# Attention and a two-part mixture of experts on one core: the second layer's first weights loaded behind the sixth head pair's keys, with new instruction orders for the attention part

## The chip, the core and the metric

The kernel runs on one core of a Trainium2 chip. The core has a matrix engine (PE, or TensorE), a vector engine (DVE), a scalar engine (ACT), GpSimd (POOL) and SyncE (SP), whose queue here issues nearly all DMA transfers. Each engine works through its own list in order; semaphores hold an instruction until what it needs is there. The metric is the device time of one execution in microseconds (us).

## The reference

What is computed, cut to what matters:

```
scores = scale * q @ k.T                       # 2 batches, 8 heads, 576 tokens, 64 per head
scores = where(0 <= i - j < 128, scores + bias, -1e9)   # a sliding window with slopes per head
attn = softmax(scores);  x = (attn @ v) laid out as [1152, 512]
out = 0                                        # first mixture: 4 experts, 512 -> 1024 -> 512
for e in range(4):
    out += p[:, e:e+1] * (relu(x @ w1[e]) @ w2[e])
xn = out / rms(out) * rms_g                    # second block: gate, value, out
return (silu(xn @ w_gate) * (xn @ w_val)) @ w_out       # 512 -> 1536 -> 512
```

All of it is in float32; most matrix products are done as three products of a rounded high part and a low part (the remainder).

## The kernel before, in words

The program has two parts. The first is the attention with some of the first expert's work between; the second is all the rest, ordered by a planner (`Plan`). The change touches the first part alone, and the instructions of the second part stand in the same order on every engine in both kernels.

Attention goes by head pairs, numbered 0 to 7 (four of batch 0, then four of batch 1). A pair's steps are:

- `load` (line 392): SP issues the pair's queries and keys (lines 403, 404) into one of two `qt`/`kt` buffers, and with every second pair the values of two pairs (lines 409, 410). A pair's buffers are those of the pair two before it, so the transfer waits until that pair's last scores are done.
- scores on PE (line 483), three pieces a pair; masked minimum on DVE (503); exponential on ACT (509); sums turned into factors on DVE (526, 527, once for three rows of blocks); scaling of each block on POOL (532), nine a pair.
- transposes on PE (550), copies of them out by DVE or ACT (388, 390), products with the values on PE (569 and 580).
- `halves` (597): ACT writes the high part, DVE the low part of the result.

Between these stand the first weights of the two layers of expert 0. `weights` (610) loads two transfers of 512 KB into the two buffers `raw` (`load_raw`, 260). ACT writes a high part of each half (388), and POOL or DVE the low part (629), so a layer has four low parts, two for each `raw` buffer. The second layer's two loads need the `raw` buffers back: the first after low parts 1 and 2 of the first layer, the second after low parts 3 and 4.

As soon as batch 0 is done, products of the first layer (654) and then of the second (685) fill PE between the transposes of batch 1.

What sets the order: `Flow` (line 151). Every operation is added with its possible engines, a cost and its needs. A string for each engine (`ORDERS`: d DVE, a ACT, p POOL, t PE) says which kind comes next there; `SHARED` says which engine takes an operation that two could do. SP's loads stand in the order in which they were added. `Flow.run` walks the strings with the costs and emits the operations by the start times that it finds; the hardware then holds each engine to the list that comes out.

In `weights`, a load is told to need `prev["w"]`, which is the second low part of the layer before, and then only for the first of the two loads (line 621 sets it to nothing). The second load is given no need.

Of the kernel before, what the change touches and what calls it, by code (L numbers as in the profile page):

```python
# [150 lines left out]
class Flow:  # L151
# [17 lines left out]
    def run(self, orders, shared):  # L169
# [30 lines left out]

ORDERS = {
    "d": (
        "bbbbmmmmmmmrmmmrmmmrmcmrcmmmcrmmmrmlmmmhrmmmcrcmrcmclmhcmrmmmrmmmcmmrclhmcmmmrcmmmmrmhlmummcmrWrummu"
        "rmcmcmurcmmmmrluuruumhucWmmmprumgummrcgmmlhyrmgrcclgucuhyculh"
    ),
    "a": (
        "mmmmmmmmmmmmmmmcmmcmmhlmmcmcmmmmmmmwlhwmmcmmmcmmhlwmmwmcmcmmhlmmmmwmmmwvwmmmmvmucvmwmmmvlhmcmvmvmmcc"
        "umvvgcmumglmmgmhmgmcmclcyhccuhlyvv"
    ),
    "p": "BnnnnnnnnnBnnnBnnnnnnnnnnnnnnWWnnnnnnnnnnWWnnnnnnnnnnnnnnnnWnnnnnnnnnnWnnnnnnnnnn",  # L210
    "t": (
        "ssssssxsxxoxxooozsxxssxxoooxxozssxxoosxxooxzssxxooxxsoozssxfffsfxffxfxfxsoooozssxfffxfxffxfxfoooozss"
        "xggggxgxgxgxgoooozxgxgxggxgxgoooozggkjkj"
    ),
}
SHARED = {
    "B": "ppp",
    "W": "ppppdpdp",
    "c": "ddadaaadddddaadddaadddddaadaaadaaddaadda",
    "y": "dada",  # L220
}


# [1 line left out]
def tile_fused(ctx: ExitStack, tc: tile.TileContext, qS, kS, vS, probs, w1, w2, wgv, wo, g, out):  # L225
# [19 lines left out]
    def slot_a():  # L245
        return wpa.tile([P, 2, 512], F32R, tag="wa", name="wa")
# [11 lines left out]
    def load_raw(src):  # L258
        raw = wraw.tile([P, 2, 512], F32, tag="raw", name="raw")
        nc.sync.dma_start(out=raw, in_=src)  # L260
        return raw
# [50 lines left out]
    def load_probs():  # L312
        nc.sync.dma_start(out=pr_sb, in_=probs)

    def norm_probs():
        nc.vector.tensor_reduce(out=psm, in_=pr_sb, op=ALU.add, axis=mybir.AxisListType.X)
        nc.vector.tensor_scalar(out=psm, in0=psm, scalar1=1e-9, scalar2=None, op0=ALU.add)
        nc.vector.reciprocal(out=psm, in_=psm)
        nc.vector.tensor_tensor(out=pn_sb, in0=pr_sb, in1=psm.to_broadcast([P, NTT, E]), op=ALU.mult)

    y = ypool.tile([P, NTT, DM], F32, tag="y", name="y")
# [18 lines left out]
    with (  # L340
# [38 lines left out]
        order = [(b, p) for b in range(B) for p in range(H // 2)]  # L379
        flow = Flow({"t": 3.9, "d": 1.6, "a": 2.9, "p": 4.15, "q": 0.7})  # L380
        add = flow.add
        qts, kts, vts, sts, pts, pes, pos = {}, {}, {}, {}, {}, {}, {}
        sps, psts, raws = {}, {}, {}
        did = {}

        def copied(e, out, in_):
            if e == "a":
                nc.scalar.activation(out=out, in_=in_, func=AF.Copy)
            else:
                nc.vector.tensor_copy(out, in_)  # L390
# [4 lines left out]
        def load(n):  # L395
            b, p = order[n]

            def both(e):
                if n not in qts:
                    qts[n] = qk_p.tile([P, S], F32, tag="q", name="qt")  # L400
                    kts[n] = qk_p.tile([P, S], F32, tag="k", name="kt")
                for c in ((slice(0, FIRST), slice(FIRST, S)) if n == 0 else (slice(0, S),)):
                    (nc.scalar if n == 0 else nc.sync).dma_start(out=qts[n][:, c], in_=qS[b, p, :, c])
                    nc.sync.dma_start(out=kts[n][:, c], in_=kS[b, p, :, c])

            def values(e):
                vt = v_p.tile([P, 5, 4 * D], F32, tag="v", name="vt")
                hs = slice(p * P - P, p * P - P + 4 * D)
                nc.sync.dma_start(out=vt[:, :4, :], in_=vS[b, : 4 * P, hs].rearrange("(k p) d -> p k d", p=P))
                nc.sync.dma_start(out=vt[:D, 4, :], in_=vS[b, 4 * P :, hs])  # L410
                vts[n - 1] = vts[n] = vt

            hold, took = (2.0, 3.9) if n == 0 else (1.5, 3.5)
            did["qk", n] = add("q", "q", (hold, took), [did.get(("s", n - 2, 8))], both)
            did["qa", n] = did["qk", n]
            if n == 0:
                did["qa", 0] = add("q", "q", (0.0, 1.3), [], lambda e: None)
            if p % 2:
                did["v", n - 1] = did["v", n] = add("q", "q", (1.5, 3.7), [did.get(("o", n - 4, 4)), did.get(("o", n - 3, 4))], values)
            if n == 0:  # L420
                for i in range(2):
                    for r in range(2):
                        rows = slice(r * D, (r + 1) * D)

                        def slopes(e, rows=rows, r=r, i=i):
                            nc.vector.tensor_scalar(
                                out=bias[rows, 0, i, :], in0=rel[rows], scalar1=-8.0 * 2.0 ** (-8.0 * ((r ^ i) + 1) / H),
                                scalar2=1.0, op0=ALU.mult, op1=ALU.mult,
                            )

                        did["b", 0, r, i] = add("b", "d", (0.33, 0.4), [did["rel", r]], slopes)
            elif b == 0:

                def steeper(e):
                    EN[e].tensor_scalar(
                        out=bias[:, p, :, :], in0=bias[:, p - 1, :, :], scalar1=2.0 ** (-16.0 / H),
                        scalar2=1.0, op0=ALU.mult, op1=ALU.mult,
                    )

                cost = {"d": (0.48, 0.55), "p": (0.75, 0.8)}  # L440
                j = add("B", "dp", cost, [did["b", p - 1, r, i] for r in range(2) for i in range(2)], steeper)
                for r in range(2):
                    for i in range(2):
                        did["b", p, r, i] = j
# [168 lines left out]
        def weights(name, srcs, behind):  # L613

            made, ends = blocks.setdefault(name, []), []
            for i, src in enumerate(srcs):
                def fetch(e, i=i, src=src):
                    raws[name, i] = load_raw(src)

                j = add("q", "q", (1.35, 3.7), [behind, prev["w"]], fetch)  # L620
                prev["w"] = None
                for k in range(2):
                    def high(e, i=i, k=k):
                        made.append(slot_a())
                        copied(e, made[2 * i + k][:, 0, :], raws[name, i][:, k, :])

                    def low(e, i=i, k=k):
                        w = made[2 * i + k]
                        EN[e].tensor_tensor(out=w[:, 1, :], in0=raws[name, i][:, k, :], in1=w[:, 0, :].bitcast(F32), op=ALU.subtract)

                    ja = add("w", "a", (0.52, 0.62), [j, prev["wa"]], high)
                    prev["wa"] = ja
                    ends.append(add("W", "dp", {"p": (1.25, 1.29), "d": (0.62, 0.7)}, [ja], low))
            prev["w"] = ends[1]
            return ends

        def bank_of(rota):
# [94 lines left out]
            keep(3, 0, [j4])  # L732

        prev = dict.fromkeys("sxowf")
        prev["wa"] = None
        load(0)
        for n in range(len(order)):
            if n + 1 < len(order):
                load(n + 1)
            for ts in SCORES:  # L740
                scores(n, ts)
                for t in ts:
                    softmax(n, t)
            for t0 in range(0, NQ, 3):
                norm(n, t0, t0 + 3)
            for kb in range(5):
                values(n, kb)
            halves(n)
            if n == 2:
                did["w1"] = weights("w1_0", [w1[0, 0], w1[0, 1]], did["qk", 3])  # L750
                j = add("q", "q", (0.5, 3.5), [did["qk", 3]], lambda e: load_probs())
                did["pn"] = add("p", "d", (0.7, 0.8), [j], lambda e: norm_probs())
            if n == 3:
                did["w2"] = weights("w2_0", [w2[0, :, :2, :], w2[0, :, 2:, :]], did["qk", 4])
                x0 = [did[w, i] for w in ("ld", "hd") for i in range(4)]
                hid = [hidden_filler("ff", c, t0, (x0 + did["w1"], [])) for c in range(4) for t0 in (0, HT)]
                for t in range(4):
                    out_filler(t, hid)
                sums(x0, hid[-1])
# [36 lines left out]
    def add(e, out, a, b):  # L796
        EN[e].tensor_tensor(out=out, in0=a, in1=b, op=ALU.add)  # L797
# [410 lines left out]
    w, v = blocks.pop("w1_0"), blocks.pop("w2_0")  # L1208
# [18 lines left out]
    v = [((lambda x=x: x), End(0.0)) for x in v]  # L1227
# [66 lines left out]
    for u in range(1, NU):  # L1294
        w, w_read = nxt
# [130 lines left out]
    for e in (ET.PE, ET.DVE, ET.Activation, ET.Pool, ET.SP):  # L1426
        prev = None
        for i in traced[mark : listed if e == ET.SP else None]:
            if i.engine == e:
# [5 lines left out]
                prev = i  # L1435
# [32 lines left out]
```

## Time and profile before

| | us |
|---|---|
| median of 3 runs (lowest, highest) | 663.32 (661.49, 663.57) |
| the profiled execution, its own time | 663.5 |
| its span, first to last instruction | 661.7 |
| PE busy in the span | 647.8 (98%) |
| DVE busy | 509.0 (77%) |
| ACT busy | 314.9 (48%) |
| POOL busy | 45.8 (7%), all in the first 80 us |

The span is one execution taken by the profiler. Its own time is 1.8 us longer, since it holds what lies before the first and behind the last instruction. A matmul's end is modelled, so that gaps between the starts tell more than busy time. The granted clock is the share of full speed that the throttle gave PE: 1.00 is 2.4 GHz and 0.50 is 1.2 GHz.

### The profile page before, as it was taken

What the parts mean: (1) busy time and instruction counts of PE and PEld (TensorE: products, weight loads), DVE (VectorE), ACT (ScalarE), POOL (GpSimd) and SP (SyncE); (2) the same over time, 40 slices, a digit from 0 to 9 for tenths busy, and PEclk for the clock granted to TensorE, in tenths of its full rate; (3) what the DMA queues carried; (4) which work ended last, traced back from release to release, by engine and by line L of the source; (5) the groups of instructions that cost most, each with busy time, mean ns of one, the idle gap of its engine ahead of it and who ended that gap; (6) DMA issues with size and microseconds to landing.
All of it is one profiled execution on the core that took longest, in us unless ns stands there. A gap on an engine that the chain in (4) does not pass through costs nothing.

```text
span 661.7 us, 11029 instructions
## 1 busy us (share of the span) xinstructions
PE 647.8 (98%) x4166; PEld 583.8 (88%) x4166; DVE 509.0 (77%) x1116; ACT 314.9 (48%) x722; POOL 45.8 (7%) x95
## 2 busy tenths in 40 slices
PE   8879999999999999999999999999999999999997
PEld 5568798988989989989989889879998999889986
DVE  7858758688888888888888888889677378857672
ACT  7957555552543634625544534864355334313330
POOL 7735300000000000000000000000000000000000
PEclk9979999999999999999999999999999999999999
DMA  8251103324452543644515434012101201001012
GB/s 275 88 198 34 33 1 108 115 96 144 144 175 96 188 140 95 216 126 139 189 47 194 134 95 160 33 41 86 65 33 60 68 1 64 23 11 33 33 49 95
DMA packets 24229, 64.95 MB, mean 98 GB/s; under 512 B 2672, under 2 KB 5488, under 8 KB 24176
## 3 DMA queue, kind: packets, MB, share of 16 engines
q1 hardware_dynamic: 23888, 63.96, 29.9%
q8 instruction: 32, 0.52, 0.3%
q10 hardware_dynamic: 288, 0.30, 0.1%
q14 instruction: 21, 0.17, 0.1%
HBM read 52.45 MB, written 11.80 MB: 97 GB/s over the span
## 4 chain that ended last, share of the span: by engine, by line
PE 96%; DMA 2%; DVE 1%; POOL 1%; SPq 0%; issue 0%; ACT 0%; POOLq 0%
PE ps_a L1167 14%; PE ps_c L1049 11%; PE ps_d L1049 11%; PE ps_d L1167 9%; PE ps_c L1167 9%; PE ps_b L1167 8%; PE ps_b L1049 8%; PE ps_a L1049 8%; PE a L654 2%; PE ps_b L285 2%; PE ps_c L285 2%; PE ps_d L285 2%; PE ps_a L285 2%; PE pst L550 2%; PE po L569 2%; PE a L685 2%
## 5 line engine op out<-in xcount | busy, mean ns | idle before, releaser
L1167 PE MATMUL ps_a<-wa,op 128*128 128x512 f32 x396 | 93.8, 390 | 0.0
L1167 PEld LDWEIGHTS ps_a<-wa,op 128*128 128x128 f32 x396 | 74.2, 188 | 15.3
L801 ACT ACTIVATE op<-h 128x512 fp32r<-128x512 f32 x95 | 57.6, 626 | 59.5 <-PE ps_d L1167 24.7
L801 ACT ACTIVATE wb<-raw 128x512 fp32r<-128x512 f32 (+1 forms) x98 | 49.8, 536 | 39.5 <-DVE raw L794 39.4
L794 DVE TENSOR_TENSOR op<-h,op 128x512 fp32r<-128x512 f32 x95 | 63.7, 685 | 2.5 <-ACT op L801 2.2
L1167 PE MATMUL ps_c<-wa,op 128*128 128x512 f32 x252 | 59.1, 389 | 0.0
L1167 PE MATMUL ps_d<-wa,op 128*128 128x512 f32 x252 | 58.9, 389 | 0.0
L1167 PE MATMUL ps_b<-wa,op 128*128 128x512 f32 x240 | 56.6, 391 | 0.0
L794 DVE TENSOR_TENSOR wb<-raw,wb 128x512 fp32r<-128x512 f32 (+1 forms) x98 | 54.6, 576 | 2.1 <-ACT wb L801 1.7
L1167 PEld LDWEIGHTS ps_c<-wa,op 128*128 128x128 f32 x252 | 47.3, 188 | 9.8
L1167 PEld LDWEIGHTS ps_d<-wa,op 128*128 128x128 f32 x252 | 47.2, 188 | 9.8
L1167 PEld LDWEIGHTS ps_b<-wa,op 128*128 128x128 f32 x240 | 44.6, 188 | 9.1
L794 DVE TENSOR_TENSOR wa<-raw,wa 128x512 fp32r<-128x512 f32 (+1 forms) x50 | 32.0, 652 | 13.5 <-ACT wa L801 13.5
L1049 PE MATMUL ps_c<-xh,wb 128*128 128x288 f32 x160 | 38.6, 297 | 0.0
L1049 PE MATMUL ps_d<-xh,wb 128*128 128x288 f32 x160 | 38.6, 296 | 0.0
L1049 PE MATMUL ps_a<-xh,wb 128*128 128x288 f32 x160 | 38.3, 294 | 0.0
L1049 PE MATMUL ps_b<-xh,wb 128*128 128x288 f32 x160 | 38.2, 294 | 0.0
L801 ACT ACTIVATE wa<-raw 128x512 fp32r<-128x512 f32 (+1 forms) x50 | 28.0, 597 | 18.9 <-DMA raw<-in_w 16.5
L1110 ACT ACTIVATE h<-r 128x576 f32<-128x576 f32 x28 | 19.2, 685 | 30.9 <-DVE r L797 30.9
L797 DVE TENSOR_TENSOR r<-ps_c,x 128x288 f32<-128x288 f32 x44 | 20.1, 458 | 17.0 <-PE ps_c L1049 14.5
L794 DVE TENSOR_TENSOR raw<-raw 128x256 f32<-128x256 f32 x66 | 27.7, 419 | 0.7
L1049 PEld LDWEIGHTS ps_b<-xh,wb 128*128 128x128 f32 x160 | 27.8, 188 | 0.3
(264 smaller groups left out, 1531.6 us busy)
## 6 DMA issues: line engine op xcount, KB each, us to landing
raw<-in_w SPq DMA_DIRECT2D x32, 512.0 KB, 3.8
scratch<-in_wgv SPq DMA_DIRECT2D x24, 512.0 KB, 4.4
f<-stage SPq DMA_DIRECT2D x36, 256.0 KB, 2.5
raw<-f SPq DMA_DIRECT2D x18, 512.0 KB, 3.2
scratch<-in_wo SPq DMA_DIRECT2D x12, 512.0 KB, 4.6
out_y<-acc SPq DMA_DIRECT2D x9, 256.0 KB, 2.0
vt<-in_vS SPq DMA_DIRECT2D x4, 512.0 KB, 6.0
qt<-in_qS SPq DMA_DIRECT2D x7, 288.0 KB, 3.3
```

What stands on the lines that cost most here:

```text
L285: nc.tensor.matmul(ps, lhsT=a, rhs=x[:, k, tok], start=(n == 0), stop=(n == 3 * KC - 1))
L550: nc.tensor.transpose(pst[:w, j, :], tts[n % 2][:, 2 * kb + j, c0 : c0 + w], ident)
L569: nc.tensor.matmul(po[r, kb * P : kb * P + len(range(blocks.shape[1])) * P], lhsT=vt[:, kb, v], rhs=blocks[:, :, 1:3, :] if j else blocks[ ...
L654: nc.tensor.matmul(box[0], lhsT=a, rhs=x[:, k, tok], start=k == 0 and a is wh and x is xh, stop=k == 3 and a is wl)
L685: nc.tensor.matmul(box[0], lhsT=tile[0][:, x, k, :], rhs=v[:, i, :], start=k == 0 and x == i == 0, stop=k == 3 and x == 1)
L794: EN[e].tensor_tensor(out=out, in0=a, in1=b, op=ALU.subtract)
L797: EN[e].tensor_tensor(out=out, in0=a, in1=b, op=ALU.add)
L801: nc.scalar.activation(out=out, in_=a, func=AF.Copy)
L1049: nc.tensor.matmul(ps, lhsT=s[:, k, :], rhs=t(k), start=start and m == 0, stop=m == 5, skip_group_check=True,)
L1110: return wrote(gr, pl.now("a", tok.stop - tok.start, needs + was_reading[gr], lambda e: nc.scalar.activation(out=h[:, c, tok], in_=src, fu ...
L1167: nc.tensor.matmul(ps, lhsT=a(s)[:, k, :], rhs=w[k][0]()[:, i, :], start=(n == 0), stop=(n == 11))
```

## The change

Three things are done. The sixth pair's load (pair 5) is added ahead of the second layer's weights, and these get it as their `behind`. Both loads of the second layer are told of both low parts that free their buffer (`prev["w"][2 * i : 2 * i + 2]`). The loads of queries, keys and values are given longer times to landing (`took`), and the strings of all engines are others. Of the strings the first lines of two are shown.

```diff
@@ ORDERS, SHARED
-    "p": "BnnnnnnnnnBnnnBnnnnnnnnnnnnnnWWnnnnnnnnnnWWnnnnnnnnnnnnnnnnWnnnnnnnnnnWnnnnnnnnnn",
+    "p": "BBnnnnnnnnnBnnnnnnnnnnnnnnnnnnnnnWnnnWnnnWnnnnnnnnnnWnnnnnnnnnnnnnWnnnnnnnnnnnnn",
-    "W": "ppppdpdp",
+    "W": "pdpppddp",
...
@@ load
-            hold, took = (2.0, 3.9) if n == 0 else (1.5, 3.5)
+            hold, took = (2.0, 3.9) if n == 0 else (1.5, 4.4 if n == 1 else 4.1)
...
-                did["v", n - 1] = did["v", n] = add("q", "q", (1.5, 3.7), [did.get(("o", n - 4, 4)), did.get(("o", n - 3, 4))], values)
+                did["v", n - 1] = did["v", n] = add("q", "q", (1.5, 4.3), [did.get(("o", n - 4, 4)), did.get(("o", n - 3, 4))], values)
@@ weights
-                j = add("q", "q", (1.35, 3.7), [behind, prev["w"]], fetch)
-                prev["w"] = None
+                j = add("q", "q", (1.35, 3.7), [behind, *prev["w"][2 * i : 2 * i + 2]], fetch)
...
-            prev["w"] = ends[1]
+            prev["w"] = ends
@@ the loop over the pairs
-        prev["wa"] = None
+        prev["wa"], prev["w"] = None, []
         load(0)
         for n in range(len(order)):
-            if n + 1 < len(order):
+            if n + 1 < len(order) and n != 4:
                 load(n + 1)
+            if n == 3:
+                load(5)
+                did["w2"] = weights("w2_0", [w2[0, :, :2, :], w2[0, :, 2:, :]], did["qk", 5])
...
             if n == 3:
-                did["w2"] = weights("w2_0", [w2[0, :, :2, :], w2[0, :, 2:, :]], did["qk", 4])
                 x0 = [did[w, i] for w in ("ld", "hd") for i in range(4)]
```

SP's list, from pair 4's queries to pair 6's keys. In the kernel before, `qt_425` and `kt_426` are pair 4, `raw_495` and `raw_525` the second layer's weights, `qt_548`, `kt_549` pair 5, `vt_578` the values of pairs 4 and 5, `qt_601`, `kt_602` pair 6:

```order
L403 DMA qt_425<-in_qS 128x576
L404 DMA kt_426<-in_kS 128x576
L260 DMA raw_495<-in_w2 128x1024
L260 DMA raw_525<-in_w2 128x1024
L403 DMA qt_548<-in_qS 128x576
L404 DMA kt_549<-in_kS 128x576
L409 DMA vt_578<-in_vS 128x4x256
L410 DMA vt_578<-in_vS 64x256
L403 DMA qt_601<-in_qS 128x576
L404 DMA kt_602<-in_kS 128x576
```

The same stretch of SP's list in the changed kernel, where pair 5 is `qt_482`, `kt_483` with the values `vt_564`, the weights are `raw_588` and `raw_611`, and pair 6 is `qt_631`, `kt_632`:

```order
L403 DMA qt_452<-in_qS 128x576
L404 DMA kt_453<-in_kS 128x576
L403 DMA qt_482<-in_qS 128x576
L404 DMA kt_483<-in_kS 128x576
L409 DMA vt_564<-in_vS 128x4x256
L410 DMA vt_564<-in_vS 64x256
L260 DMA raw_588<-in_w2 128x1024
L260 DMA raw_611<-in_w2 128x1024
L403 DMA qt_631<-in_qS 128x576
L404 DMA kt_632<-in_kS 128x576
```

Four transfers of pair 5 have moved from behind the two weight transfers to a place ahead of them; pair 6's stand behind the weights in both.

POOL's list around pairs 2 to 4 in the kernel before; the `st` buffers tell the pairs apart (`st_321` is pair 2, `st_397` pair 3, `st_523` pair 4), and the rows of line 629 are the first layer's low parts, two for each of `raw_374` and `raw_399`:

```order
L532 TENSOR_SCALAR tt_122<-tt_122,st_321 128x192 x6
L629 TENSOR_TENSOR wa_441<-raw_374,wa_441 128x512
L629 TENSOR_TENSOR wa_468<-raw_374,wa_468 128x512
L532 TENSOR_SCALAR tt_122<-tt_122,st_321 128x192
L532 TENSOR_SCALAR y_87<-y_87,st_397 128x64
L532 TENSOR_SCALAR y_87<-y_87,st_397 128x128
L532 TENSOR_SCALAR y_87<-y_87,st_397 128x192 x7
L629 TENSOR_TENSOR wa_565<-raw_399,wa_565 128x512
L629 TENSOR_TENSOR wa_588<-raw_399,wa_588 128x512
L532 TENSOR_SCALAR tt_122<-tt_122,st_523 128x64
```

The same pairs in the changed kernel, where `st_320`, `st_391` and `st_538` are pairs 2, 3 and 4, and line 628 is line 629 of before:

```order
L532 TENSOR_SCALAR tt_122<-tt_122,st_320 128x192 x7
L532 TENSOR_SCALAR y_87<-y_87,st_391 128x64
L532 TENSOR_SCALAR y_87<-y_87,st_391 128x128
L532 TENSOR_SCALAR y_87<-y_87,st_391 128x192
L628 TENSOR_TENSOR wa_492<-raw_401,wa_492 128x512
L532 TENSOR_SCALAR y_87<-y_87,st_391 128x192 x3
L628 TENSOR_TENSOR wa_509<-raw_424,wa_509 128x512
L532 TENSOR_SCALAR y_87<-y_87,st_391 128x192 x3
L628 TENSOR_TENSOR wa_519<-raw_424,wa_519 128x512
L532 TENSOR_SCALAR tt_122<-tt_122,st_538 128x64
```

Three low parts of the first layer are left on POOL, and two of them now stand between the scalings of pair 3; the fourth has gone to DVE.

PE's list around pair 5's first scores (`kt_549`) in the kernel before, with the transposes of pair 3 (`y_87`) and its products (`pt_552`, `pe_553`):

```order
L569 MATMUL po_591<-pt_552,vt_347 64x256 x4
L550 MATMUL pst0_124<-ident_81,y_87 64x128
L550 MATMUL pst0_124<-ident_81,y_87 128x128 x2
L550 MATMUL pst1_125<-ident_81,y_87 64x128
L483 MATMUL s2_156<-kt_549,qt_548 64x64 x2
L483 MATMUL s0_154<-kt_549,qt_548 64x128 x2
L483 MATMUL s2_156<-kt_549,qt_548 64x192 x2
L483 MATMUL s0_154<-kt_549,qt_548 64x192 x2
L569 MATMUL po_591<-pt_552,vt_347 64x256 x2
L569 MATMUL po_591<-pt_552,vt_347 64x128 x2
L580 MATMUL pst1_125<-pt_552,vt_347 64x64 x2
```

The same place in the changed kernel, with `kt_483` for pair 5's keys and `pt_545` for pair 3:

```order
L569 MATMUL po_591<-pt_545,vt_369 64x256 x2
L550 MATMUL pst0_124<-ident_81,y_87 64x128
L550 MATMUL pst0_124<-ident_81,y_87 128x128 x2
L550 MATMUL pst1_125<-ident_81,y_87 64x128
L483 MATMUL s2_156<-kt_483,qt_482 64x64 x2
L483 MATMUL s0_154<-kt_483,qt_482 64x128 x2
L483 MATMUL s2_156<-kt_483,qt_482 64x192 x2
L483 MATMUL s0_154<-kt_483,qt_482 64x192 x2
L569 MATMUL po_591<-pt_545,vt_369 64x256 x4
L569 MATMUL po_591<-pt_545,vt_369 64x128 x2
L580 MATMUL pst1_125<-pt_545,vt_369 64x64 x2
```

Pair 5's first scores stand at the same place, but for two products of pair 3, which come behind them now.

## Rows read from the trace of the kernel before

**Rows 1.** The page, busy time of PE (share of the span, instructions).

```profile
PE 647.8 (98%) x4166; PEld 583.8 (88%) x4166; DVE 509.0 (77%) x1116; ACT 314.9 (48%) x722; POOL 45.8 (7%) x95
```

**Rows 2.** Waits of PE, 0 to 150 us: us in total, times, longest.

```profile
PE s L483 <- DMA kt<-in_kS: 7.5, 2, 6.3
PE s L483 <- DVE st L503: 0.6, 1, 0.6
```

**Rows 3.** Windows, 31 to 43 us: length, busy by engine, PEclk, DMA share, GB/s.

```profile
31.00:37.00 6.00, 0.00 (x0) 0.00 (x0) 0.56 (x4) 1.04 (x5) 1.07 (x3) 0.87 0.81 257
37.00:39.00 2.00, 1.95 (x20) 1.24 (x22) 0.68 (x5) 0.00 (x0) 0.00 (x0) 0.50 1.04 365
39.00:41.00 2.00, 2.00 (x28) 1.69 (x28) 1.09 (x7) 1.05 (x3) 1.23 (x3) 0.50 0.05 18
41.00:43.00 2.00, 2.00 (x20) 1.49 (x13) 1.44 (x6) 2.00 (x10) 0.00 (x0) 0.70 0.00 0
```

**Rows 4.** The chain of waits through the stall: start us, us, what.

```profile
28.40 2.49 POOL wa L629 x2
...
30.91 0.33 SPq L260
...
31.76 5.16 DMA kt<-in_kS
...
37.05 1.35 PE s L483 x12
38.40 1.48 PE po L569 x8
39.88 0.52 PE pst L580 x6
...
40.50 1.88 PE s L483 x18
42.38 0.56 PE pst L550 x4
```

**Rows 5.** The same chain elsewhere, at full clock.

```profile
20.61 0.32 PE pst L580 x6
...
21.63 0.32 PE a L483 x5
...
22.95 1.01 PE po L569 x8
23.96 0.70 PE s L483 x12
...
47.02 0.44 PE pst L550 x4
...
49.47 0.80 PE a L654 x6
...
65.37 0.97 PE s L483 x18
```

**Rows 6.** SP's queue in order of time: start us, us, what it issued.

```profile
23.66 7.57 SPq L260 DMA_DIRECT2D raw<-in_w  x2
31.33 0.38 SPq L403 DMA_DIRECT2D qt<-in_qS  x1
```

**Rows 7.** POOL in order of time, 21 to 31 us, idle before in brackets.

```profile
21.13 2.51 POOL L629 TENSOR_TENSOR wa<-raw,wa 128x512 fp32r<-128x512 f32 x2
...
27.17 1.23 POOL L532 TENSOR_SCALAR y<-y,st 128x192 f32<-128x192 f32 x3 [0.43 <-ACT xh L603]
28.36 2.52 POOL L629 TENSOR_TENSOR wa<-raw,wa 128x512 fp32r<-128x512 f32 x2
```

**Rows 8.** Lines 526 and 629: ns min/median/max, first and last start; one in time order.

```profile
L526 DVE TENSOR_SCALAR st<-st x24: 152/166/682, 6.8 to 72.0; 128x3 f32<-128x3 f32 x24
L629 POOL TENSOR_TENSOR wa<-raw,wa x6: 1267/1280/1702, 21.1 to 64.5; 128x512 fp32r<-128x512 f32 x6
...
30.22 0.68 DVE L526 TENSOR_SCALAR st<-st 128x3 f32<-128x3 f32 x1
```

More of the change, by code (lines that the diff above doesn't have):

```diff
@@ L202 @@
     "d": (
-        "bbbbmmmmmmmrmmmrmmmrmcmrcmmmcrmmmrmlmmmhrmmmcrcmrcmclmhcmrmmmrmmmcmmrclhmcmmmrcmmmmrmhlmummcmrWrummu"
-        "rmcmcmurcmmmmrluuruumhucWmmmprumgummrcgmmlhyrmgrcclgucuhyculh"
+        "bbbbmmmmmmmrmmrmmmmmrmmmccrrmmcmmmmcmmrmmlrmhrmcmmcrmmrmlmhccmrWccmmmmrlhmmmmrcmmmmrmhlmumruurmuumum"
+        "mmmrmrummWhlucumrcmprmWmmmmcgrgluhgmmcrmrmmccrlhcycucuguhul"
     ),
     "a": (
-        "mmmmmmmmmmmmmmmcmmcmmhlmmcmcmmmmmmmwlhwmmcmmmcmmhlwmmwmcmcmmhlmmmmwmmmwvwmmmmvmucvmwmmmvlhmcmvmvmmcc"
-        "umvvgcmumglmmgmhmgmcmclcyhccuhlyvv"
+        "mmmmmmmmmmmmmmmmmcmmmmmmlhcmmcmmmmcmmlhcmwmwwmwmmclhmmccmmcmmhmlmmwmmwvccmmvummvmccmmchmvmmlmmcwvuwv"
+        "mmvmcvmcgmmglgmhmmmcmygmmulhcchuylyvv"
     ),
-    "p": "BnnnnnnnnnBnnnBnnnnnnnnnnnnnnWWnnnnnnnnnnWWnnnnnnnnnnnnnnnnWnnnnnnnnnnWnnnnnnnnnn",
+    "p": "BBnnnnnnnnnBnnnnnnnnnnnnnnnnnnnnnWnnnWnnnWnnnnnnnnnnWnnnnnnnnnnnnnWnnnnnnnnnnnnn",
     "t": (
-        "ssssssxsxxoxxooozsxxssxxoooxxozssxxoosxxooxzssxxooxxsoozssxfffsfxffxfxfxsoooozssxfffxfxffxfxfoooozss"
-        "xggggxgxgxgxgoooozxgxgxggxgxgoooozggkjkj"
+        "ssssssxxssxxoooxxozsssxxoxxooozxsxxoooxxsxozssxxoxxsooozssxfxffffxfxffxsoooozssfxfxffxfxffxfxsoooozs"
+        "sgxgxggxggxoooozxggxgxgxgxoooozgggggkjkj"
     ),
@@ L217 @@
     "B": "ppp",
-    "W": "ppppdpdp",
-    "c": "ddadaaadddddaadddaadddddaadaaadaaddaadda",
-    "y": "dada",
+    "W": "pdpppddp",
+    "c": "ddaddaaddaaddddaaaadaaaaaaddadadadddadda",
+    "y": "adaa",
 }
```

## The prediction, made before the changed kernel ran

> **What bounds the kernel now.** I read the page first: PE is busy for 647.8 of the span's 661.7 us [rows 1], so no other engine bounds the whole, and what can be won is PE's 13.9 us of gaps and any time at a low clock. Next PE's waits [rows 2]: after the start there are 7.5 us for a transfer of keys, in two waits, the longest 6.3 us, and one of 0.6 us for DVE. Nothing later waits. Then the windows around the long wait [rows 3]: from 31 to 37 us PE does nothing, DVE, ACT and POOL almost nothing, and the DMA engines are 81% busy; from 37 to 41 PE works at a granted clock of 0.50, that is 1.2 GHz, and from 41 to 43 at 0.70 in the mean.
>
> The chain says why [rows 4]. POOL does two low parts of the first layer's weights, to 30.89. Then SP, which had stood at the second weight transfer of line 260, issues it, and behind it pair 5's queries and keys; the keys take 5.16 us to land, and pair 5's first scores start at 37.05. SP's own rows say the same [rows 6]: its two weight loads fill 23.66 to 31.23, since they wait for their buffers, and pair 5's queries are issued only at 31.33. So keys that depend on nothing but pair 3's last scores, done at 21.63 + 0.32 = 21.95 [rows 5], are 9.4 us late behind a transfer that nobody needs yet.
>
> **The change part by part.** I work against the profiled execution's own 663.5 us (span 661.7 and 1.8 around it); the median of the runs shown is 663.32, 0.2 below.
>
> *Pair 5 ahead of the weights.* PE came to the stall at 37.05 - 6.30 = 30.75. In the changed list it comes there about 0.5 earlier, since two products of pair 3 (half of the 1.01 us that eight records take [rows 5]) now follow the scores: 30.2. The keys can be issued from 21.95 on; issue to start of the scores took 37.05 - 31.33 = 5.7 us in the crowded stretch [rows 4, 6], with the values right behind, as they are again. That gives 27.7, 2.5 us in time. The wait of 6.3 us goes as a whole: -6.3.
>
> *The clock.* The four long pieces after the stall took 1.35, 1.48, 0.52 and 1.88 us [rows 4]; the same pieces at full clock take 0.70, 1.01, 0.32 and 0.97 [rows 5]. The differences are 0.65 + 0.47 + 0.20 + 0.91 = 2.2 us. What PE did before the fall was to stand still for 6.3 us; the 0.6 us wait early on lowered nothing that a chain row shows. Without the stall this goes too: -2.2. The bounds are 0, if some other gap brings the clock down, and 2.6, which is half the time below full clock in the windows (2 x 2.0 x 0.5 + 2.0 x 0.3 [rows 3]).
>
> *The new strings on PE.* The same instructions, in another order. Each change between scores, transposes, products and fillers costs something: four transposes take 0.56 us behind scores and 0.44 behind a filler [rows 4, 5], a difference of 0.12. Counted over the strings there are 77 such changes before and 73 after, so at most 4 x 0.12 = 0.5 us is won; the kinds are mixed, and a costlier one could take their place. I take -0.2, between -0.5 and +0.5.
>
> *What is late next.* In the stall DVE, ACT and POOL stood too [rows 3], having no more to do; they were hardly behind PE when it began. Without it they must feed pair 3's last transposes and pair 4's first at PE's pace. Two edits touch this. Two of the first layer's low parts, 1.28 us each [rows 8], now stand on POOL between pair 3's scalings, where before they came in front of (21.13 to 23.64) and behind (from 28.36) them [rows 7]. PE needs those scalings for the transposes just before pair 5's scores. But ahead of pair 3's last scaling there are two low parts in both lists, so POOL has done the same work by then, and before it was idle for 0.43 us on the way [rows 7]. And DVE takes one low part from POOL in this stretch; its own price for one isn't among the rows, so I bound it by POOL's 1.28 [rows 8]. What PE sees of all this is bounded below by nothing, since the list before kept PE going with a single wait of 0.6 us from 7 to 30.75 [rows 2], and above by two low parts, 2 x 1.28 = 2.6, if both lie bare in front of a transpose. I take the nearest row, one wait of 0.6: +0.6.
>
> Here a rule of the Trainium skill speaks against the change. The reduction of three sums to factors (line 526) takes 166 ns as a rule and once 682 [rows 8]; that one began at 30.22 and ended at 30.90 [rows 8], while POOL was in a low part that ended at 30.89 [rows 4]. SBUF — State Buffer, section "Who interferes with whom", says that the vector engine and GpSimd share a pair of ports by an exclusive lock, and that the later one waits for a whole instruction. By the rows the loss is 0.5 us for such a meeting; by the rule it could be nearly all of POOL's instruction. Three low parts now stand close to three such reductions (pairs 3 and 4); if each met one at 0.5 us and all of it reached PE, the sum would be 1.5 higher instead of 0.6.
>
> *Pair 6 behind the weights.* Its transfers now have the place that pair 5's had. The second weight load waits for the third and fourth low parts, and the last of these is POOL's, behind pair 3's scalings as before, where it ended at 30.89 [rows 4]. Low part's end to scores was 37.05 - 30.89 = 6.2 us, so pair 6's keys are there at about 37. PE wants them later: 30.2, the rest of pair 3 and pair 5's other scores (0.70 + 1.4 + 0.3 + 1.0 = 3.4 from [rows 5]), four transposes 0.56, eight fillers of 0.80 (the row of 0.80 is one filler [rows 5]) and twelve more transposes at 0.11, 1.3: 41.9. That is 5 us in time; cost 0. The cover is those fillers; if it were gone, each us of lateness would cost one.
>
> *The second layer's weights.* They land some 1 to 3 us later at most, and their products come only after pair 5's own, tens of us later: 0. *The longer `took` values* are only numbers for the walk: 0. *The second part* has the same order on every engine and PE waits nowhere in it [rows 2]: it starts earlier by what the first part wins and loses none of it.
>
> Sum: 663.5 - 6.3 - 2.2 - 0.2 + 0.6 = 655.4 us.
>
> **The rivals.** *A: part of the stall comes back as a wait on POOL, DVE or ACT.* For it: two low parts are placed among pair 3's scalings, and reductions can be held at the port. Against it: POOL has one low part less in all and waited for DVE and ACT before [rows 7]. Price: two bare low parts (2.6) and three held reductions (3 x 0.5) in place of the 0.6, and, if the gap lowers the clock, up to 2.2 more: 658.3 to 661, 659 in the middle.
>
> *B: the change doesn't do what it says.* Pair 5's keys still come late, since their transfer meets the values and the weights (the DMA engines were full at 37 to 39 [rows 3]), or SP is held elsewhere. They would have to land 2.5 us later than I work out. If a third of the wait stayed (2 us) it would be 657.5; if all of it, no change, 663.
>
> *C: slower, the same wait one pair later.* Pair 6's keys are now behind the wait that held pair 5's. It decides from the point where POOL's last low part of the first layer ends after 41.9 - 6.2 = 35.7 us instead of near 31. From there each us counts once, and the clock's 2.2 comes back. At an end of 43.5 us it would be 655.4 + 7.8 + 2.2 = 665.4. For it: only POOL's list and its place behind nine scalings. Against it: POOL's work before this point is less by one low part, so something would have to hold POOL for 12 us; the only waits of that kind were for the stall itself.
>
> **How the numbers follow.** A measurement of this kernel can tell 0.3%, 2.0 us, from no change. The forecast, the stall gone with at most a small wait in its place, has 0.75 and lies between 653.3 (655.4 less the 0.6, the remaining 0.3 of the changes of kind, the other 0.4 of the clock's bound and as much again for the run) and 657.6 (655.4 plus 2.0 of the larger bound for the waits, and 0.2). Rival A has 0.13 and B 0.08, of which 0.03 is left unchanged; C has 0.04. The range goes from 653.3 to 659.5, which takes in the middle of A and the smaller case of B. Faster: 0.75 + most of A (0.11) + 0.05 of B = 0.91; same: 0.02 + 0.03 = 0.05; slower: 0.04.
>
> **What would show it right or wrong.** In the profile of the changed kernel SP issues pair 5's queries near 22 us and the weights behind them; PE's waits have no row of several us for `kt`; the granted clock stays at 1.00 from 25 to 45 us; pair 5's first scores start near 30; the first product of the second part (line 285) starts some 8 us earlier than before. It would be wrong if PE's waits show rows for POOL, DVE or ACT of more than 2.6 us together between 25 and 45 us (A), if the keys land after 31 (B), or if a wait of PE for `kt` appears at pair 6's first scores (C).

## The result and the profile after

| | before | changed |
|---|---|---|
| median, us (lowest to highest, 4 runs each) | 662.82 (661.49 to 663.57) | 655.00 (654.84 to 655.43) |
| ratio of the times, 95% interval | | 0.9885 (0.9867 to 0.9903) |
| profiled execution, its own time | 663.5 | 655.43 |
| span | 661.7 | 653.7 |

The changed kernel is 1.15% faster, and the profiled executions differ by 8.07 us. The forecast was 655.4.

PE's waits of the changed kernel, 0 to 150 us (us in total, times, longest); the second of them, 1.2 us for DVE's memset, belongs to the kernel's start:

```profile
PE s L483 <- DVE st L503: 2.0, 2, 1.7
PE ps L358 <- DVE y L354: 1.2, 1, 1.2
```

The 6.3 us for `kt` of [rows 2] are gone. The other 1.2 us of that row stood at pair 1's first scores, where PE still waits. But for 0.12 us, what is left stands in the first 11 us, as PE's list in order of time shows (idle before in brackets):

```profile
7.97 0.82 PE L483 MATMUL s<-kt,qt 64*64 64x64 f32 x18 [1.70 <-DVE st L503]
10.94 0.82 PE L483 MATMUL s<-kt,qt 64*64 64x64 f32 x18 [0.34 <-DVE st L503]
```

Before, the same two places had 1.18 and 0.56 us. The profile names DVE, but the keys of pairs 1 and 2 landed at 7.83 and 10.80, and PE starts 0.14 us after each. In all nine traces every gap of PE from 5 to 13 us ends 0.13 to 0.14 us after the landing of these keys: they are waits for keys, whatever the profile names. SP's queue of the changed kernel answers to [rows 6] (start us, us, what it issued):

```profile
22.33 0.33 SPq L403 DMA_DIRECT2D qt<-in_qS  x1
22.70 0.43 SPq L404 DMA_DIRECT2D kt<-in_kS  x1
...
25.71 5.51 SPq L260 DMA_DIRECT2D raw<-in_w  x2
31.32 0.38 SPq L403 DMA_DIRECT2D qt<-in_qS  x1
```

Pair 5's queries go out at 22.33 instead of 31.33. SP still stands at the second weight load, for nearly the whole of 5.51 us, and now it is pair 6's queries that follow at 31.32. The chain of waits runs through PE from 10.94 us on, but for 0.12 us; its pieces around pair 5's first scores answer to [rows 4]:

```profile
26.14 0.12 issue
...
30.76 0.70 PE s L483 x12
31.46 1.23 PE po L569 x12
32.70 0.32 PE pst L580 x6
...
33.07 0.97 PE s L483 x18
34.04 0.56 PE pst L550 x4
...
42.28 0.90 PE s L483 x16
```

The scores of 1.35 and 1.88 us are back at 0.70 and 0.97. The last row holds pair 6's first scores: their queries were issued 11 us before. The windows answer to [rows 3] (length, busy by engine, PEclk, DMA share, GB/s):

```profile
32.00:37.00 5.00, 5.00 (x63) 4.49 (x60) 4.43 (x17) 4.48 (x18) 2.67 (x6) 1.00 0.90 298
37.00:39.00 2.00, 2.00 (x18) 1.98 (x17) 0.70 (x4) 2.00 (x8) 0.94 (x2) 1.00 1.02 333
39.00:41.00 2.00, 2.00 (x19) 1.98 (x17) 1.33 (x3) 2.00 (x8) 1.94 (x3) 1.00 0.18 63
```

PE is never idle there and the granted clock stays at 1.00, with the DMA engines as full from 32 to 39 us as before: their traffic costs PE nothing that shows here.

POOL and DVE beside each other, in the stretch where two low parts stand between pair 3's scalings; first POOL, then DVE's reductions of line 526 (start us, us):

```profile
23.54 1.28 POOL L628 TENSOR_TENSOR wa<-raw,wa 128x512 fp32r<-128x512 f32 x1 [0.49 <-ACT wa L388]
...
26.71 1.26 POOL L628 TENSOR_TENSOR wa<-raw,wa 128x512 fp32r<-128x512 f32 x1
...
29.60 1.27 POOL L628 TENSOR_TENSOR wa<-raw,wa 128x512 fp32r<-128x512 f32 x1
```

```profile
24.36 0.48 DVE L526 TENSOR_SCALAR st<-st 128x3 f32<-128x3 f32 x1
...
27.14 0.85 DVE L526 TENSOR_SCALAR st<-st 128x3 f32<-128x3 f32 x1
...
30.72 0.18 DVE L526 TENSOR_SCALAR st<-st 128x3 f32<-128x3 f32 x1 [0.53 <-ACT tt L509]
```

Two of the three reductions were held, to 24.84 and 27.99, just when POOL's low part ended (24.82 and 27.97). The chain shows no wait of PE beside them, but for the 0.12 us at 26.14.

### The profile page after: what moved, and what is told of

It reads as the page before. It is cut to its first block, busy times and chain, and to the rows that moved or that the text cites. A ratio compares the mean times of both kernels' runs of the same rounds, so it can differ in the third digit from the quotient of the medians.

```text
span 653.7 us, 11039 instructions
## 1 busy us (share of the span) xinstructions
PE 645.7 (99%) x4166; PEld 583.5 (89%) x4166; DVE 506.2 (77%) x1114; ACT 316.4 (48%) x725; POOL 43.4 (7%) x94
## 4 chain that ended last, share of the span: by engine, by line
PE 98%; DVE 1%; issue 0%; ACT 0%
PE ps_a L1168 14%; PE ps_c L1050 11%; PE ps_d L1050 11%; PE ps_d L1168 9%; PE ps_c L1168 9%; PE ps_b L1168 8%; PE ps_b L1050 8%; PE ps_a L1050 8%; PE a L653 2%; PE ps_b L285 2%; PE ps_c L285 2%; PE pst L550 2%; PE ps_d L285 2%; PE ps_a L285 2%; PE po L569 2%; PE a L684 2%
```

## The experiments

The comparisons are with runs of the kernel before on the same chip: median 662.90 us for the load order alone, the strings alone, no wait for buffers and the first attempt to keep PE busy, 663.07 for the other three.

**The load order alone.** The kernel before with pair 5's load ahead of the weights and every string as it was:

```diff
-            if n + 1 < len(order):
+            if n + 1 < len(order) and n != 4:
                 load(n + 1)
             ...                                  # scores and softmax of pair n
+            if n == 3:
+                load(5)
+                did["w2"] = weights("w2_0", [w2[0, :, :2, :], w2[0, :, 2:, :]], did["qk", 5])
             ...
-                did["w2"] = weights("w2_0", [w2[0, :, :2, :], w2[0, :, 2:, :]], did["qk", 4])
```

> The kernel before with one part of the change: pair 5's load ahead of the second layer's weights, all engine strings as before. Theory (the stall was SP's order, and the strings are worth next to nothing): PE has no wait of several us for kt near 30 us, the granted clock stays at 1.00, and the time is 654.5 to 657. Rival (the new strings bring the gain, since without them DVE, ACT or POOL come late): 658 to 663, with waits of PE for these engines of more than 2.6 us between 25 and 45 us.

Measured: 655.65 us (655.40 to 656.57), ratio 0.9888 (0.9876 to 0.9901). PE's only gaps behind the memset:

```profile
7.00 0.82 PE L483 MATMUL s<-kt,qt 64*64 64x64 f32 x18 [1.19 <-DVE st L527]
10.82 0.77 PE L483 MATMUL s<-kt,qt 64*64 64x64 f32 x16 [1.38 <-DVE st L503]
```

From 11 us on there is none, with the old strings too. They were as good as the new ones for feeding PE. Measured each against its own runs of the kernel before, the two kernels can't be told apart (0.9888 and 0.9885), and their profiled executions took 655.40 and 655.43 us, although this one waits 0.5 us longer in the first 11 us.

**The strings alone.** The changed kernel with its strings and needs, the weights ahead of pair 5 again:

```diff
-            if n + 1 < len(order) and n != 4:
+            if n + 1 < len(order):
                 load(n + 1)
             if n == 3:
-                load(5)
-                did["w2"] = weights("w2_0", [w2[0, :, :2, :], w2[0, :, 2:, :]], did["qk", 5])
+                did["w2"] = weights("w2_0", [w2[0, :, :2, :], w2[0, :, 2:, :]], did["qk", 4])
```

> The changed kernel with its new strings and needs, but with the weights ahead of pair 5's load on SP as before. Theory: the low part that frees the second buffer ends near 30.9 us, the queries follow at 31.3, pair 5's first scores start near 37, so PE waits about 6.3 us, the clock falls to 0.50 and costs 2.2 more: 662.5 to 664.5. Rival (the strings bring the gain): 655 to 658.

Measured: 663.05 us (662.25 to 663.62), ratio 0.9999 (0.9990 to 1.0007). SP stood at the weights and issued pair 5's queries at 31.02; PE's waits:

```profile
PE s L483 <- DMA kt<-in_kS: 7.9, 3, 5.8
```

The stall is back with the order, 5.8 us of it instead of the 6.3 expected, and from 37 to 41 us the granted clock is 0.50 again. With the first experiment this divides the gain: all of it, as far as can be measured, is SP's order; the strings alone are worth nothing.

**No wait for buffers.** The kernel before, SP's order and strings as they were, but the first layer's weights land in `y`'s rows 0 to 3, which nobody uses then, so that both `raw` buffers are empty for the second layer's:

```diff
-                    raws[name, i] = load_raw(src)
+                    if name == "w1_0":
+                        raws[name, i] = y[:, 2 * i : 2 * i + 2, :]
+                        nc.sync.dma_start(out=raws[name, i], in_=src)
+                    else:
+                        raws[name, i] = load_raw(src)
```

> The kernel before with SP's order and all strings as they were, but the first layer's weights land in four rows of y that are free then, so that the second layer's two loads find empty raw buffers. Theory (the stall was the wait for buffers, not the place in the order or the bytes ahead): both weight loads go out near 18 us, pair 5's queries near 22, and PE has no wait for kt near 30 us: 654.5 to 657. Rival (1 MB ahead in the queue is what makes the keys late): they land after 31 and PE waits 1 to 4 us, with the clock lowered again: 657 to 662.

Measured: 654.79 us (654.62 to 657.29), ratio 0.9882 (0.9868 to 0.9896). SP's queue:

```profile
17.80 0.90 SPq L260 DMA_DIRECT2D raw<-in_w  x2
21.99 0.33 SPq L403 DMA_DIRECT2D qt<-in_qS  x1
22.36 0.43 SPq L404 DMA_DIRECT2D kt<-in_kS  x1
```

PE's last gap in the first 150 us is this one:

```profile
10.15 0.77 PE L483 MATMUL s<-kt,qt 64*64 64x64 f32 x16 [0.66 <-DMA kt<-in_kS]
```

The weights are still ahead of the keys, 1 MB of them, and PE waits for nothing from 11 us on. So the place in the order alone makes no stall; the wait for a buffer at the head of an in-order queue does. That the bytes ahead cost nothing is not shown: the weights went out 4 us before the queries, and the keys still took 4.2 us to land, against 3.0 in the changed kernel, only early enough. This is another way to the same time: the ratios 0.9882 and 0.9885 can't be told apart. The one execution of 657.29 us had a granted clock of 0.996 over its span where the other three had 1.000; its cause is open.

**Half of the order back.** The changed kernel with the first of the two weight loads ahead of pair 5, the second behind:

```diff
-        def weights(name, srcs, behind):
+        def weights(name, srcs, behind, between=None):
...
+                if i and between:
+                    between()
...
-                load(5)
-                did["w2"] = weights("w2_0", [w2[0, :, :2, :], w2[0, :, 2:, :]], did["qk", 5])
+                did["w2"] = weights("w2_0", [w2[0, :, :2, :], w2[0, :, 2:, :]], did["qk", 4], lambda: load(5))
```

> The changed kernel with the first of the two weight loads put back ahead of pair 5's load; the second stays behind. Theory (what counts is when the buffer comes free, and by how much that passes the margin): the first load goes out near 25.7 us, pair 5's queries near 26.1, the scores could start 5.7 us later at 31.8, PE is there at 30.7, so it waits about 1.1 us for kt; a gap of that size lowers no clock: 655.5 to 656.7. Rival 1 (the margin is larger than that): no wait, 654.8 to 655.4. Rival 2 (any such gap brings the clock down): 657.5 to 659.

Measured: 655.74 us (655.45 to 656.27), ratio 0.9887 (0.9870 to 0.9903). The queries went out at 25.68 and PE's scores of pair 5 were late by less than half of what I had worked out:

```profile
30.71 0.77 PE L483 MATMUL s<-kt,qt 64*64 64x64 f32 x16 [0.42 <-DVE st L527]
```

The profile names a reciprocal that ended at 30.64, but these scores read nothing of it. The keys, issued at 26.10, landed at 30.58, and the scores started 0.13 us later, just as in the kernel before (landing 36.92, start 37.05 [rows 4]): it was the keys. Issue of the queries to scores was 5.0 us instead of 5.7. How long pair 5's keys took from their issue to landing, in the changed kernel, with no wait for buffers, and here (KB, us):

```profile
kt<-in_kS SPq DMA_DIRECT2D x1, 288.0 KB, 3.0
kt<-in_kS SPq DMA_DIRECT2D x1, 288.0 KB, 4.2
kt<-in_kS SPq DMA_DIRECT2D x1, 288.0 KB, 4.5
```

In the kernel before it was 5.16 [rows 4]. Over all nine traces it was 3.0 to 4.1 us in the three kernels that issue pair 5 ahead of the weights, and 4.2 to 5.3 in the six with weights ahead of it. So the weights' bytes seem to have made up some 1 to 2 of the 6.3 us of the stall (an estimate, 5.2 - 4.1 and 5.2 - 3.0; no run tried it by itself), and the wait for the buffer the rest. In the changed kernel the keys landed at 25.70, so the margin before PE came at 30.69 is 5.0 us, not 2.5. The clock stayed at 1.00 over the gap. The wait was 0.42 us instead of 1.1, and the time decides nothing between the theory and rival 1: the ratios 0.9887 and 0.9885 can't be told apart.

**PE kept busy in the stall, first attempt.** The kernel before with products in front of pair 5's first scores, into the bank that these write next:

```diff
+                if (n, ts[0]) == (5, 0):
+                    for _ in range(22):
+                        nc.tensor.matmul(bank[own[0]][:, :P], lhsT=ident, rhs=ident, start=True, stop=True)
```

> The kernel before with 22 products of the identity with itself put in front of pair 5's first scores; their result is written over by the scores. Theory (the low clock after the stall comes from PE's standing still, and costs 2.2 us): the products fill 4 to 6 us of the stall, pair 5's first scores still start near 37, the granted clock stays at 1.00 from 25 to 45 us, and the time is 2 us under the kernel before, 660 to 661.5. Rival (the pieces after the stall are slow for another reason, such as the DMA traffic): the scores of line 483 still take 1.35 and 1.88 us, and the time is that of before, 662 to 664.

Measured: 663.91 us (661.77 to 665.07), ratio 1.0008 (0.9997 to 1.0019). The time lies in the rival's range, but the scores of line 483 (line 487 here) took 0.96 and 1.43 us, neither the theory's values nor the rival's. PE's list and the chain:

```profile
30.63 5.08 PE L481 MATMUL s<-ident 128*128 128x128 f32 x44
38.34 0.96 PE L487 MATMUL s<-kt,qt 64*64 64x64 f32 x16 [2.64 <-DMA kt<-in_kS]
```

```profile
39.30 1.48 PE po L573 x8
40.78 0.52 PE pst L584 x6
...
41.40 1.43 PE s L487 x18
```

The keys came 1.3 us later here (SP's issue of the queries took 1.56 us instead of 0.38; why is open), so a gap of 2.64 us stayed, and the granted clock still fell to 0.50, here from 39 to 42 us. This profile alone settles nothing, but the times do. The twelve executions fall into two groups by their granted clock over the whole span: seven at 0.996 or 0.997, the profiled one among them, took 663.85 to 665.07 us (median 664.24), and five at 0.999 or 1.000 took 661.77 to 662.36 (median 662.15). So one and the same kernel, with the clock's fall and without it, differs by 2.1 us, next to the 2.2 predicted. Why the clock fell in some of them and not in others is open, since only one has a trace.

**PE kept busy, second attempt.** 19 products of the dense `bias` tile instead, 128x192 each:

```diff
-                        nc.tensor.matmul(bank[own[0]][:, :P], lhsT=ident, rhs=ident, start=True, stop=True)
+                        nc.tensor.matmul(bank[own[0]][:, :WIN], lhsT=bias[:, 0, 0, :P], rhs=bias[:, 1, 0, :], start=True, stop=True)
```

> The kernel before with 19 products of the dense bias tile (128x192 each) in front of pair 5's first scores, which write over them. The 22 identity products took 5.1 us and left a gap of 2.6 us, and the clock fell all the same. Theory (PE's standing still lowers the clock, and the low clock costs 2.2 us): the products fill 6 to 7 us from about 30.7, the gap before the scores is under 1.5 us, the granted clock stays at 1.00, the scores, products and scores behind the stall take about 0.70, 1.0 and 0.97 us, and the time is 660 to 662. Rival (those pieces are slow for another cause): they take 1.35, 1.48 and 1.88 us again, and the time is 662.5 to 664.

Measured: 662.28 us (660.88 to 663.55), ratio 0.9986 (0.9976 to 0.9995), between the theory's range and the rival's; the profiled span was 660.6. The chain behind the stall and the windows over it:

```profile
38.29 0.77 PE s L487 x12
39.06 0.80 PE po L573 x8
39.86 0.32 PE pst L584 x6
...
40.24 0.97 PE s L487 x18
```

```profile
32.00:37.00 5.00, 5.00 (x33) 4.96 (x31) 0.00 (x0) 0.36 (x2) 0.58 (x2) 1.00 0.83 248
37.00:39.00 2.00, 0.97 (x20) 0.47 (x18) 0.00 (x0) 0.00 (x0) 0.00 (x0) 1.00 0.95 283
39.00:41.00 2.00, 2.00 (x38) 1.65 (x36) 1.74 (x11) 1.09 (x5) 0.65 (x2) 1.00 0.64 243
```

With PE at work until 37.26 the clock stays at 1.00, and the four pieces take 2.86 us instead of 5.23, although the keys landed about 1.2 us later and the DMA engines were as full as before. So the slow pieces were the clock's doing, and the clock's fall came of PE's standing still. By the clock and by the pieces the theory holds, though its time was missed by 0.3 us. The size, 2.2 us by [rows 4, 5], is 2.4 here. The time gained less because of the later keys: 2.4 - 1.2 = 1.2 by the profiles; the medians differ by 0.8.

**The held reductions.** The changed kernel without the addition in front of the reciprocal, which leaves out the 1e-9:

```diff
-                nc.vector.tensor_scalar(out=st[:, 2, gs], in0=st[:, 1, gs], scalar1=1e-9, scalar2=None, op0=ALU.add)
-                nc.vector.reciprocal(out=st[:, 3, gs], in_=st[:, 2, gs])
+                nc.vector.reciprocal(out=st[:, 3, gs], in_=st[:, 1, gs])
```

> The changed kernel without the addition of 1e-9 before the reciprocal (line 526, 24 instructions, two of them held to 0.48 and 0.86 us beside POOL's low parts); it leaves that addition out. Theory (DVE's held reductions lie beside PE's work and cost nothing from 11 us on; only those in the first 11 us stand in PE's way): the waits of PE for DVE near 8 and 11 us shrink by 0.2 to 0.6, nothing else moves: 654.2 to 655.1. Rival (the holds at the shared ports reach PE): 652.5 to 654.

Measured: 654.53 us (654.21 to 655.09), ratio to the kernel before 0.9867 (0.9852 to 0.9881). The reciprocal takes the addition's place, twice in the middle of a low part of POOL (it began at 24.16 and 26.94, the low parts lasted from 23.33 to 24.62 and from 26.23 to 27.50), and isn't held (ns min/median/max):

```profile
L526 DVE RECIPROCAL st<-st x24: 163/172/178, 7.3 to 64.3; 128x3 f32<-128x3 f32 x24
```

PE waits 0.59 and 0.48 us in the first 11 us and nowhere after, against 0.12 us after 11 in the changed kernel. So from 11 us on the holds cost PE 0.12 us at the very most. The 0.5 us in the median are of the size of what the first 11 us vary by from one execution to another, and I make nothing of them. The part of the theory on those waits was wrong: they were for keys, which landed at 7.33 and 10.60 here, so the addition didn't stand in PE's way there either.

## Why the prediction was right, point by point

- **The stall goes as a whole: right.** 6.3 us of waiting for `kt` became none. Pair 5's queries were issued at 22.33 (21.95 predicted) and PE came to the scores at 30.69 (30.2 predicted; 0.4 us of the difference is what the start took longer). One term was mis-sized without harm: by the 5.7 us of the crowded stretch the keys were to be 2.5 us in time, and they were 5.0, since they landed in 3.0 us from their issue and not in 5.2. That it was SP's order, and in it the buffer wait, is shown from both sides: the order alone gives the whole gain, the strings alone none, and the old order without the buffer wait gives the whole gain again.
- **The clock, 2.2 us: right.** The pieces are back at their full-clock times, and the two fillings of the stall show cause and size by themselves: 2.4 us in the pieces of the second, 2.1 between the two groups of executions of the first.
- **The strings, -0.2, and new waits, +0.6: each wrong by a little, their sum right.** PE's gaps behind the memset went from 1.18 + 0.56 = 1.74 to 1.70 + 0.34 + 0.12 = 2.16, that is +0.4. The ledger 6.30 + 2.23 - 0.42 = 8.11 against a measured 8.07 leaves 0.04 for the strings, so four changes of kind less were worth nothing that shows. That the two errors cancel is luck. Nor did the +0.6 come from where I put it, DVE, ACT or POOL being late around pair 3: there the changed kernel waits 0.12. It lies in the first 11 us, where PE waits for the keys of pairs 1 and 2 and kernels with the same lists also differ (0.7 to 2.6 us of gaps over the executions profiled here). The row from which the 0.6 was taken, a wait put down to DVE [rows 2], was such a wait too: pair 2's keys landed at 10.03, and PE went on at 10.17.
- **The rule against the change: right in the mechanism, without a price.** SBUF — State Buffer, "Who interferes with whom" in the Trainium skill, lets the later of the two engines wait for the other's whole instruction; the trace agrees, two of three reductions ended within 0.02 us of POOL's low part, one held to 0.85 us. Over a usual 0.16 the two lost 0.32 and 0.69 us, about 1.0 together, where I had let rival A have 1.5, and of that at most 0.12 reached PE. "As a rule 166 and once 682" was read too quickly from a median: in the trace of the kernel before, eight more of the 24 took 0.23 to 0.38 us, and each ended within 0.03 us of an instruction of POOL, seven of a scaling (line 532) and one of a low part. The scalings hold them too, for less.
- **Pair 6 behind the weights, cost 0: right.** Its queries went out at 31.32 (about 31.3 predicted) and its scores started at 42.28 (41.9 predicted); the keys landed at 36.23, 6 us early. Rival C's point, POOL's last low part ending after 35.7, was far off: it ended at 30.87.
- **Two sums that don't come out.** The terms named for the lower end of the range, 0.6, 0.3, 0.4 and as much again, give 653.7 and not 653.3. Rival A's price, 655.4 - 0.6 + 2.6 + 1.5, is 658.9 and not 658.3. Neither bears on the result.
- **The second part: right.** It starts as much earlier as the whole ends. Its first product, before and then changed:

```profile
88.61 0.29 PE L285 MATMUL ps_b<-xh,wa 128*128 128x288 f32 x1
```

```profile
80.53 0.29 PE L285 MATMUL ps_b<-xh,wa 128*128 128x288 f32 x1
```

These are 8.08 us, and the times differ by 8.07.

## What to carry to other kernels

When the bounding engine waits for a transfer, look at the issuing queue before the transfer: here the keys were issued 9.4 us late, behind an instruction that waited for a buffer, while the landing took 5.2 us behind a weight transfer and 3.0 in the changed kernel without one. Such a wait can be mended by order (what is needed first, first) or by a buffer (rows of a tile that is idle then); either gives the same, and neither needs the other engines' lists to change. And a gap on PE of some us is worth more than its length, since the pieces behind it run at half the clock: 6.3 us cost 8.5.

## What the runs showed of the hardware that I had not expected

- PE's clock fell to 0.50 around a gap of only 2.64 us that followed 5.1 us of identity products, and by the mean clocks it did so in seven of twelve executions of that kernel. Gaps of 1.03 us behind dense products and of up to 1.92 us near 8 us (the strings alone) left it at 1.00. Whether the length of the gap or the kind of product made the difference was not tried apart.
- The issue of one DMA on SP between 15 and 45 us usually took 0.33 to 0.6 us, but single ones took longer: 1.56 and 1.33 us in the two kernels that kept PE busy, which put the keys 1.2 to 1.3 us later, but also 1.08 in the changed kernel and 1.47 without the wait for buffers. The cause stays open.
- A reciprocal of the same three elements, in the place of the addition, was never held (178 ns at most), though two of the 24 began while POOL was in a low part; the addition was held there to 481 and 855 ns.
